# Seven weight tiles of a one-core mixture-of-experts kernel move by 32 to 416 bytes

## The chip, the cores and the metric

The kernel runs on one core of a Trainium2 chip. The metric is the device time of one execution in microseconds; lower is better. In the rows, PE is the matrix engine (TensorE), PEld its weight loads, DVE the vector engine, ACT the scalar engine, POOL GpSimd, SP the engine that issues most transfers.

## The reference, cut to what matters

```python
x = retention(q, k, v)             # 2304 tokens x 512, decayed causal attention without softmax
P = sinkhorn(exp(x @ w_gate))      # 8 rounds of row and column scaling, 2304 x 8
for e in range(8):                 # first layer: every token through every expert
    out += P[:, e:e+1] * (relu(x @ w1[e]) @ w2[e])      # w1 512 x 1024, w2 1024 x 512
logits = out @ moe2_w_gate         # second layer: only the expert with the largest logit
out2[t] = softmax(logits[t])[e] * (relu(out[t] @ w1b[e]) @ w2b[e])
```

## The kernel before, in words

Four stages follow one another: the attention, pass 1 of the first layer, pass 2 of it, and the second layer (class `Top1`). In pass 1 and pass 2 a unit `u` is half of one expert (512 of its 1024 hidden columns), so there are 16 units in each pass. Every factor is split into a high and a low part (`...h`, `...l`, 32-bit), and a product is taken as three matmuls: high with high, low with high, high with low.

The hidden layer of one unit, for 1024 tokens, is made by `Dense.hidden` with seven block products in place of eight. Product `i` multiplies the weight block `w{a}` with the token block `op{b}`, where `PROD` gives `(a, b)`. A weight tile is 128 x 2 x 256 values, 2048 bytes in each of the 128 rows of the on-chip memory; a token tile is 128 x 1024, 4096 bytes. `product` issues six matmuls for each of two column blocks `p`: two depth halves `k`, three matmuls in each. The weights (128 columns, 512 bytes a row) are loaded into the array, and 512 token columns (2048 bytes a row) stream past them. Every matmul brings its own weight load. Per unit these are 7 x 2 x 6 = 84 matmuls, so 2688 over the 32 units. They write `pha`, `phb` and `phc` (L609).

In pass 1, 256 further tokens use the same weight tiles in `rest_hidden` (`phr`, L706, 256 columns, 48 matmuls a unit, 768 in all). `y_tile` (L731) then multiplies the hidden values with `w2`: here a 128-column slice of `hhi` or `hlo` is the weight and `w2hi` or `w2lo` streams, 512 columns at a time.

All tiles of the seven products come out of pools that are laid one behind another. Before the change, `op0h` to `op6l`, `w0h` to `w6l`, `w2hi`, `w2lo`, `hhi`, `hlo`, `xrh`, `xrl`, `rhi` and `rlo` all begin at an address that is 480 modulo 512 bytes, so that a weight tile and the tokens that stream past it are a multiple of 512 bytes apart. Small unused tiles (`pad0` to `pad3`) hold this.

`lg` holds the first layer's logits (128 x 18 x 8). `sinkhorn` reads it at the start of pass 1. `Router.L` (named `L2` in its pool) holds the second layer's logits; `logit_parts` writes it 128 tokens at a time in pass 2, and `choose` and `gates` read it.

Of the kernel before, what the change touches and what calls it, by code (L numbers as in the profile page):

```python
# [10 lines left out]
F32 = mybir.dt.float32  # L11
F32R = mybir.dt.float32r
# [11 lines left out]
E = 8  # L24
F = 1024
NPAIR = H // 2
NT = N // 128
# [10 lines left out]
def split_lo(eng, out, src, hi):  # L38

    return eng.tensor_tensor(out=out, in0=src, in1=hi.bitcast(F32), op=ALU.subtract)  # L40
# [345 lines left out]
class Pumped:  # L386


    def __init__(self, eng):
        self.eng, self.bg = eng, []  # L390
# [121 lines left out]
class Dense:  # L512
# [35 lines left out]

    def w1_tasks(self, u):
        nc = self.nc  # L550
        ops = self.W1[u] = [
            tuple(self.w1p.tile([128, 2, 256], F32R, name=f"w{o}{x}", tag=f"w{o}{x}") for x in "hl")
            for o in range(7)
        ]

        def q(f, k):
            return self.raw1[:, 2 * k:2 * k + 2, 256 * f:256 * f + 256]

        def split(o, f, k):
            def run():  # L560
                nc.scalar.activation(ops[o][0], q(f, k), AF.Copy)  # L561
                split_lo(nc.vector, ops[o][1], q(f, k), ops[o][0])
            return run

        def comb(out, a, b, op):
            def run():
                nc.vector.tensor_tensor(out=q(*out), in0=q(*a), in1=q(*b), op=op)  # L567
            return run

        a11, a12, a21, a22 = (0, 0), (0, 1), (1, 0), (1, 1)  # L570
        return [
            split(A11, *a11), split(A12, *a12), split(A22, *a22),
            comb(a22, a21, a22, ALU.add), split(S1, *a22),
            comb(a21, a11, a21, ALU.subtract),
            comb(a11, a22, a11, ALU.subtract), split(S2, *a11), split(S3, *a21),
            comb(a12, a12, a11, ALU.subtract), split(S4, *a12),
        ]
# [206 lines left out]
class Router:  # L784
# [5 lines left out]

    def __init__(self, tc, ctx, crow, ident, wg2, acc, x2d, res, pt):
        self.tc, self.nc, self.ident, self.acc, self.pt = tc, tc.nc, ident, acc, pt
        self.x2d, self.res = x2d, res
        nc = self.nc
        self.v = Pumped(nc.vector)
        self.pool = pool = ctx.enter_context(tc.tile_pool(name="r_sb", reuse_waits="tile", bufs=1))
        self.C = pool.tile([128, CKEEP], F32, name="crow")
        nc.scalar.dma_start(self.C, crow[:, 0:CKEEP])  # L800
        self.wg = pool.tile([128, KD, E], F32, name="wg2")
        nc.scalar.dma_start(self.wg, wg2.rearrange("(k p) e -> p k e", p=128))
        self.C16 = pool.tile([128, 3, 128], BF16, name="c16")
        with tc.tile_pool(name="r_c", reuse_waits="tile", bufs=1) as tmp:
            t = tmp.tile([128, 384], F32, name="crow_b")
            nc.scalar.dma_start(t, crow[:, CKEEP:CKEEP + 384])
            nc.vector.tensor_copy(self.C16.rearrange("p a b -> p (a b)"), t)
        self.L = pool.tile([128, NT, E], F32, name="L2")
        self.Bm = pool.tile([128, NT, 128], BF16, name="Bm")
        self.q = pool.tile([128, NT], F32, name="rq")  # L810
        self.gp = pool.tile([128, 3, NT], BF16, name="gparts")
        self.oh = [pool.tile([128, E, n], BF16, name=f"oh{n}") for n in (NEARLY, NLATE)]
        self.xt = pool.tile([128, KD, 128], F32, name="rxt")
        pool.tile([128, 8], F32, name="pad3")
        self.B = [{}, {}]

    def c(self, k):
# [518 lines left out]
def build(ctx, tc, q, k, v, moe_w_gate, moe_w1, moe_w2, moe2_w_gate, moe2_w1, moe2_w2,  # L1336
# [4 lines left out]
    x2d = dram.tile([N, DM], F32, name="x2d")  # L1341
# [3 lines left out]
    ident = const.tile([128, 128], F32, name="ident")  # L1345
    const.tile([128, 8], F32, name="pad1")
    make_identity(nc, ident)
    res = {
        "gidx0": const.tile([128, 2], U32, name="gidx0"),
        "gidx": const.tile([128, NSLOT], U32, name="gidx"),  # L1350
        "sidx": const.tile([128, NSLOT], U32, name="sidx"),
        "gate": const.tile([128, NSLOT], F32, name="gate"),
        "e0": const.tile([128, 1], I32, name="e0"),
        "eidx": const.tile([128, NSLOT], I32, name="eidx"),
        "echg": const.tile([128, NSLOT], I32, name="echg"),
        "nslot": const.tile([128, 1], I32, name="nslot"),
# [3 lines left out]
    lg = const.tile([128, NT, E], F32, name="lg")  # L1360
# [3 lines left out]
    ops = [tuple(xpool.tile([128, 1024], F32R, name=f"op{o}{x}") for x in "hl") for o in range(7)]  # L1364
# [31 lines left out]
    with ExitStack() as cx:  # L1396
# [19 lines left out]
        aux = ctx.enter_context(tc.tile_pool(name="aux", reuse_waits="tile", bufs=1, space=PSUM))  # L1416
# [35 lines left out]
    with tc.manual_schedule(engines=order):  # L1452
# [3 lines left out]
        for u in range(2 * E):  # L1456
# [20 lines left out]
            if u == 2 * E - 1:  # L1477
# [8 lines left out]
                g, w = nc.gpsimd, nc.vector  # L1486
# [17 lines left out]
                    t()  # L1504


        ro = Router(tc, ctx, c_row, ident, moe2_w_gate, acc, x2d, res, aux)
        etmp = ctx.enter_context(tc.tile_pool(name="r_early", reuse_waits="tile", bufs=1))
        for i in range(NEARLY):
            ro.store(i)  # L1510
# [53 lines left out]
    with tc.manual_schedule(engines=MANUAL):  # L1564
# [58 lines left out]
    n = nc.values_load(  # L1623
        res["nslot"][0:1, 0:1], min_val=NFULL, max_val=NSLOT,
        skip_runtime_bounds_check_because="18 to 26 slots hold 2304 tokens of 8 experts",
    )
# [40 lines left out]
```

## Time and profile before

| | |
|---|---|
| median of three runs | 2007.47 us (2002.96 to 2007.79) |
| the profiled execution's own time | 2002.13 us |
| its span, first to last instruction | 2000.3 us |
| TensorE clock granted, mean | 0.996 of 2.4 GHz |
| PE busy | 1956.9 us, 98% of the span, 9584 matmuls |
| PEld busy | 1627.4 us, 81% |
| DVE, ACT, POOL busy | 1252.1, 847.7, 298.9 us |

Matmuls are pipelined: one starts before the one ahead of it has ended, and the duration that a row gives for one (389 ns for 512 columns) is longer than the distance from its start to the next one's. What a matmul costs in a dense stretch is that distance. It is read from the start times, or from a stretch of the chain of waits divided by its count.

### The profile page before, as it was taken

To read this page: it belongs to the slowest core of one execution; us is meant where nothing else is said; L and a number is where in the kernel's file an instruction comes from. 1 tells how busy PE (TensorE), PEld (TensorE's weight loads), DVE (VectorE), ACT (ScalarE), POOL (GpSimd) and SP (SyncE) were. 2 spreads that over 40 slices of the span, in tenths; PEclk is the share of its full clock that TensorE was granted. 3 is DMA by queue.
4 is the path that set the end of the run, shared out by engine and by line. 5 is a ranking of instruction groups with operands and counts; after the bars stand their busy time and mean duration, and the time that the engine had idled before them with its cause. 6 is when DMAs were issued, how large, how long until landed. Compare 5 with 4: busy or idle time off the path is not lost.

```text
span 2000.3 us, 25444 instructions
## 1 busy us (share of the span) xinstructions
PE 1956.9 (98%) x9584; PEld 1627.4 (81%) x9584; DVE 1252.1 (63%) x2059; ACT 847.7 (42%) x1454; POOL 298.9 (15%) x250
## 2 busy tenths in 40 slices
PE   8989999999999999999999999999999999999997
PEld 7777888888888888888878888888878888777775
DVE  7897565555555555555455556555576654988886
ACT  6665424232222233323333333333333334577785
POOL 6572000000000000000000000000000001465654
PEclk9999999999999999999999999999999999999998
DMA  5621111111111110111311111111111113112755
GB/s 132 142 61 64 42 43 43 43 43 43 43 42 43 43 37 28 42 43 43 111 33 64 43 43 64 42 54 52 43 46 60 47 59 116 43 43 77 249 200 192
DMA packets 112111, 134.94 MB, mean 67 GB/s; under 512 B 62190, under 2 KB 62446, under 8 KB 111600
## 3 DMA queue, kind: packets, MB, share of 16 engines
q1 hardware_dynamic: 106960, 121.92, 19.0%
q0 software_dynamic: 3680, 11.02, 1.7%
q8 instruction: 77, 1.26, 0.3%
q10 hardware_dynamic: 1344, 0.33, 0.1%
q14 instruction: 50, 0.41, 0.1%
HBM read 182.53 MB, written 12.58 MB: 98 GB/s over the span
## 4 chain that ended last, share of the span: by engine, by line
PE 82%; DVE 8%; ACT 5%; issue 3%; DMA 1%; POOL 0%; SPq 0%; ACTq 0%; POOLq 0%; DVEq 0%
PE pyt L731 37%; PE pha L609 17%; PE phc L609 8%; PE phr L706 5%; PE phb L609 4%; PE phs L1250 4%; DVE op2l L40 2%; PE po L274 2%; PE ps L210 1%; ACT op3h L1216 1%; PE pS L236 1%; ACT op2h L1216 1%; PE rpl L832 1%; DMA raw<-in_moe_w_dram 1%; PE pgate L1381 1%
## 5 line engine op out<-in xcount | busy, mean ns | idle before, releaser
L731 PE MATMUL pyt<-w2hi,hhi 128*128 128x512 f32 x1024 | 402.5, 393 | 2.4 <-DVE xb L742 2.2
L731 PE MATMUL pyt<-w2hi,hlo 128*128 128x512 f32 x1024 | 398.9, 390 | 0.0
L731 PE MATMUL pyt<-w2lo,hhi 128*128 128x512 f32 x1024 | 398.5, 389 | 0.0
L635 ACT ACTIVATE q<-pha 128x512 f32<-128x512 f32 x192 | 114.7, 599 | 266.8 <-PE pha L609 264.4
L623 ACT ACTIVATE hhi<-q 128x512 fp32r<-128x512 f32 x192 | 121.4, 632 | 249.9 <-DVE q L631 249.9
L731 PEld LDWEIGHTS pyt<-w2hi,hhi 128*128 128x128 f32 x1024 | 192.3, 188 | 42.8 <-DVE xb L742 2.9
L731 PEld LDWEIGHTS pyt<-w2hi,hlo 128*128 128x128 f32 x1024 | 192.2, 188 | 40.7
L731 PEld LDWEIGHTS pyt<-w2lo,hhi 128*128 128x128 f32 x1024 | 192.4, 188 | 38.8
L624 DVE SCALAR_TENSOR_TENSOR hlo<-q,hhi 128x512 fp32r<-128x512 f32 x192 | 133.0, 693 | 96.8 <-ACT hhi L623 90.8
L742 DVE SCALAR_TENSOR_TENSOR xa<-pyt,P,xa 128x512 f32<-128x512 f32 x140 | 105.0, 750 | 136.0 <-PE pyt L731 135.2
L742 DVE SCALAR_TENSOR_TENSOR xb<-pyt,P,xb 128x512 f32<-128x512 f32 x120 | 90.1, 751 | 94.0 <-PE pyt L731 94.0
L631 DVE TENSOR_TENSOR q<-phb,q 128x512 f32<-128x512 f32 x64 | 44.3, 692 | 166.0 <-PE phb L609 166.0
L40 POOL TENSOR_TENSOR op2l<-xb,op2h 128x1024 fp32r<-128x1024 f32 x1 | 2.4, 2387 | 719.4 <-ACT op2h L494 719.4
L631 DVE TENSOR_TENSOR q<-phc,q 128x512 f32<-128x512 f32 x128 | 87.8, 686 | 34.0 <-PE phc L609 33.1
L561 ACT ACTIVATE w3h<-raw 128x512 fp32r<-128x512 f32 x31 | 19.6, 631 | 160.4 <-DVE raw L567 160.3
L567 DVE TENSOR_TENSOR raw<-raw 128x512 f32<-128x512 f32 x124 | 85.1, 687 | 1.1
L40 DVE TENSOR_TENSOR w2lo<-raw,w2hi 128x512 fp32r<-128x512 f32 x124 | 84.6, 683 | 0.0
L587 ACT ACTIVATE w2hi<-raw 128x512 fp32r<-128x512 f32 x124 | 77.1, 623 | 0.0
L714 DVE SCALAR_TENSOR_TENSOR rlo<-phr,rhi 128x512 fp32r<-128x512 f32 x32 | 22.1, 691 | 87.7 <-ACT rhi L713 87.7
L908 POOL TENSOR_SCALAR Bm<-c,ro 128x128 bf16<-128x128 bf16 x2 | 1.3, 653 | 456.2 <-DVE ro L408 456.2
L561 ACT ACTIVATE w4h<-raw 128x512 fp32r<-128x512 f32 x31 | 19.6, 632 | 116.2 <-DVE raw L567 116.2
L40 DVE TENSOR_TENSOR op2l<-raw,op2h 128x1024 fp32r<-128x1024 f32 x22 | 60.6, 2756 | 10.1 <-ACT op2h L1216 9.6
(391 smaller groups left out, 4765.3 us busy)
## 6 DMA issues: line engine op xcount, KB each, us to landing
raw<-in_moe_w_dram SPq DMA_DIRECT2D x180, 512.0 KB
raw<-in_moe_w_dram SPq DMA_DIRECT2D x62, 1024.0 KB
kt<-in_k_dram SPq DMA_DIRECT2D x32, 128.0 KB
vt<-in_v_dram SPq DMA_DIRECT2D x32, 128.0 KB
qt<-in_q_dram SPq DMA_DIRECT2D x32, 128.0 KB
x2d<-xa SPq DMA_DIRECT2D x10, 256.0 KB
xbd<-xb SPq DMA_DIRECT2D x1, 2048.0 KB
xb<-xbd SPq DMA_DIRECT2D x2, 1024.0 KB
```

Source lines behind the costliest of these rows:

```text
L40: return eng.tensor_tensor(out=out, in0=src, in1=hi.bitcast(F32), op=ALU.subtract)
L567: nc.vector.tensor_tensor(out=q(*out), in0=q(*a), in1=q(*b), op=op)
L587: nc.scalar.activation(hi, self.raw2[:, fc, :], AF.Copy)
L609: self.nc.tensor.matmul(bank, ww[:, k, 128 * p:128 * p + 128], xx[:, k, :], start=start and n == 0, stop=stop and n == 5, skip_group_check ...
L623: nc.scalar.activation(hi, c, AF.Relu)
L624: nc.vector.scalar_tensor_tensor(out=lo, in0=c, scalar=0.0, in1=hi.bitcast(F32), op0=ALU.max, op1=ALU.subtract)
L631: self.nc.vector.tensor_tensor(out=s, in0=p, in1=s, op=ALU.add)
L635: self.nc.scalar.activation(t, c, AF.Copy)
L706: nc.tensor.matmul(pt[:, j, :], w[:, k, 128 * j:128 * j + 128], xr[x][:, xi, k, :], start=n == 0, stop=n == 11,)
L731: nc.tensor.matmul(pt, hh, ww, start=n == 0, stop=n == 11)
L742: nc.vector.scalar_tensor_tensor(out=acc, in0=pt, scalar=P[:, i, e:e + 1], in1=acc, op0=ALU.mult, op1=ALU.add)
L1250: nc.tensor.matmul(ph, xx[:, k, :], ww[:, fs], start=n == 0, stop=n == 11)
```

## The change

Eight unused tiles are laid around the seven weight pairs. They hold 8, 8, 8, 24, 16, 16, 24 and 24 values of 4 bytes, so 32, 32, 32, 96, 64, 64, 96 and 96 bytes, 512 in all. A pair takes 4096 bytes, eight times 512, so the distance modulo 512 from a weight tile to its tokens becomes the sum of the unused tiles ahead of it:

| weight | w0 | w1 | w2 | w3 | w4 | w5 | w6 |
|---|---|---|---|---|---|---|---|
| product, tokens | 1, op0 | 2, op1 | 4, op6 | 5, op3 | 6, op4 | 7, op5 | 3, op2 |
| distance before | 0 | 0 | 0 | 0 | 0 | 0 | 0 |
| distance after, bytes | 32 | 64 | 96 | 192 | 256 | 320 | 416 |

To make room, the second layer's logits no longer have a tile of 576 bytes of their own; they are written into `lg`, and `pad3` grows by 64 bytes, so what follows the router's pool stays at its place modulo 512. No instruction is added, removed or moved on any engine, and no wait: the two programs differ in addresses, and in the name of the logits' tile.

```diff
     def w1_tasks(self, u):
         nc = self.nc
-        ops = self.W1[u] = [
-            tuple(self.w1p.tile([128, 2, 256], F32R, name=f"w{o}{x}", tag=f"w{o}{x}") for x in "hl")
-            for o in range(7)
-        ]
+        ops = self.W1[u] = []
+
+        for o, n in enumerate((8, 8, 8, 24, 16, 16, 24, 24)):
+            self.w1p.tile([128, n], F32, name=f"pad{o}", tag=f"pad{o}")
+            if o < 7:
+                ops.append(tuple(
+                    self.w1p.tile([128, 2, 256], F32R, name=f"w{o}{x}", tag=f"w{o}{x}") for x in "hl"
+                ))
...
-        self.L = pool.tile([128, NT, E], F32, name="L2")
+        self.L = L
...
-        pool.tile([128, 8], F32, name="pad3")
+        pool.tile([128, 24], F32, name="pad3")
...
-        ro = Router(tc, ctx, c_row, ident, moe2_w_gate, acc, x2d, res, aux)
+        ro = Router(tc, ctx, c_row, ident, moe2_w_gate, acc, x2d, res, aux, lg)
```

## Rows read from the trace of the kernel before

**Rows 1.** The page: the span, busy time of each engine.

```profile
span 2000.3 us, 25444 instructions
PE 1956.9 (98%) x9584; PEld 1627.4 (81%) x9584; DVE 1252.1 (63%) x2059; ACT 847.7 (42%) x1454; POOL 298.9 (15%) x250
```

**Rows 2.** The page: the chain that ended last, shares by engine and line.

```profile
PE 82%; DVE 8%; ACT 5%; issue 3%; DMA 1%; POOL 0%; SPq 0%; ACTq 0%; POOLq 0%; DVEq 0%
PE pyt L731 37%; PE pha L609 17%; PE phc L609 8%; PE phr L706 5%; PE phb L609 4%; PE phs L1250 4%; DVE op2l L40 2%; PE po L274 2%; PE ps L210 1%; ACT op3h L1216 1%; PE pS L236 1%; ACT op2h L1216 1%; PE rpl L832 1%; DMA raw<-in_moe_w_dram 1%; PE pgate L1381 1%
```

**Rows 3.** Busy time by stage: pass 1, pass 2 (columns: see first line).

```profile
core 0: us, PE busy (x) PEld busy (x) DVE busy (x) ACT busy (x) POOL busy (x), PEclk, DMA share, GB/s
190.00:1020.00 830.00, 828.70 (x4006) 699.74 (x4005) 449.08 (x725) 260.09 (x445) 10.38 (x11) 1.00 0.14 46
1020.00:1675.00 655.00, 652.38 (x2957) 540.35 (x2956) 379.97 (x608) 240.01 (x422) 2.66 (x3) 1.00 0.16 54
```

**Rows 4.** Chain of waits, one unit of pass 1 (start us, us, what).

```profile
410.99 27.20 PE pyt L731 x120
438.19 2.72 PE pha L609 x12
440.91 1.36 PE phb L609 x6
...
449.07 2.87 PE phr L706 x24
451.94 2.75 PE phc L609 x12
454.69 2.72 PE pha L609 x12
...
463.03 1.13 PE pyt L731 x5
```

**Rows 5.** Chain of waits, a part of one unit of pass 2.

```profile
1041.60 13.76 PE pyt L731 x60
1055.36 2.72 PE pha L609 x12
```

**Rows 6.** Timeline of PE after a break in pass 2 (start us, duration us).

```profile
1041.78 0.40 PE L731 MATMUL pyt<-w2lo,hhi 128*128 128x512 f32 x1
1042.02 0.40 PE L731 MATMUL pyt<-w2hi,hlo 128*128 128x512 f32 x1
1042.25 0.40 PE L731 MATMUL pyt<-w2hi,hhi 128*128 128x512 f32 x1
...
1044.10 0.39 PE L731 MATMUL pyt<-w2hi,hlo 128*128 128x512 f32 x1
```

**Rows 7.** Timeline of the weight loads at the same place.

```profile
1041.78 0.19 PEld L731 LDWEIGHTS pyt<-w2hi,hlo 128*128 128x128 f32 x1
1042.02 0.19 PEld L731 LDWEIGHTS pyt<-w2hi,hhi 128*128 128x128 f32 x1
```

**Rows 8.** Line 609: duration ns min/median/max (two of 21 alike).

```profile
L609 PE MATMUL pha<-op4h,w4l x128: 389/389/398, 182.0 to 1648.9; 128*128 128x512 f32 x128
L609 PE MATMUL pha<-op5h,w5h x128: 389/389/389, 185.9 to 1652.7; 128*128 128x512 f32 x128
```

**Rows 9.** Line 731, 1041.7 to 1043.9 us: duration ns min/median/max.

```profile
L731 PE MATMUL pyt<-w2hi,hhi x4: 393/397/486, 1041.5 to 1043.6; 128*128 128x512 f32 x4
L731 PE MATMUL pyt<-w2lo,hhi x4: 387/389/396, 1041.8 to 1043.9; 128*128 128x512 f32 x4
L731 PE MATMUL pyt<-w2hi,hlo x3: 393/395/397, 1042.0 to 1043.4; 128*128 128x512 f32 x3
```

**Rows 10.** Line 1250, from 1750 us, and `op2l`, which it waits for.

```profile
L1250 PE MATMUL phs<-op2h,xth x34: 388/388/389, 1754.1 to 1965.9; 128*128 128x512 f32 x34
L1250 PE MATMUL phs<-op2l,xth x34: 389/442/504, 1755.1 to 1966.1; 128*128 128x512 f32 x34
```

**Rows 11.** Line 1381 (8-column weights), two forms; line 706.

```profile
L1381 PE MATMUL pgate<-xa,wg x8: 379/379/383, 129.7 to 131.2; 128*8 128x256 f32 x8
...
L1381 PE MATMUL pgate<-xb,wg x16: 592/592/596, 164.8 to 177.9; 128*8 128x512 f32 x16
...
L706 PE MATMUL phr<-xrh,w0h x64: 277/283/283, 188.6 to 971.1; 128*128 128x256 f32 x64
```

**Rows 12.** Tiles `lg` and `L`: last reading of one, first writing of the other.

```profile
L427 DVE TENSOR_SCALAR sk_x<-lg,gm x1: 296/296/296, 186.0 to 186.0; 128x144 f32<-128x144 f32 x1
...
L833 ACT ACTIVATE L<-rpl x18: 158/178/179, 1042.0 to 1699.2; 128x8 f32<-128x8 f32 x18
```

**Rows 13.** The page: the two groups with the longest waits for PE.

```profile
L635 ACT ACTIVATE q<-pha 128x512 f32<-128x512 f32 x192 | 114.7, 599 | 266.8 <-PE pha L609 264.4
L623 ACT ACTIVATE hhi<-q 128x512 fp32r<-128x512 f32 x192 | 121.4, 632 | 249.9 <-DVE q L631 249.9
```

More of the change, by code (lines that the diff above doesn't have):

```diff
@@ L784, with __init__ @@
 class Router:
-    def __init__(self, tc, ctx, crow, ident, wg2, acc, x2d, res, pt):
+    def __init__(self, tc, ctx, crow, ident, wg2, acc, x2d, res, pt, L):
         self.tc, self.nc, self.ident, self.acc, self.pt = tc, tc.nc, ident, acc, pt
```

## The prediction

> **What bounds the kernel now.** I read the page first. PE is busy for 1956.9 of 2000.3 us [rows 1], and 82% of the chain that ended last is PE's; the lines of the seven products (`pha`, `phc`, `phb`) hold 17, 8 and 4% of the span, and `phr`, which shares their weights, another 5% [rows 2]. The stages come next: in pass 1 PE is busy for 828.7 of 830.0 us, in pass 2 for 652.4 of 655.0, with the granted clock at 1.00, which is the 2.4 GHz level [rows 3]. So nothing that DVE, ACT or a transfer does sets the pace there. The rows with the longest waits say the same from the other side: ACT sits idle for 264.4 us until a `pha` product is done, and 249.9 us for `q`, which DVE makes from a product [rows 13]. A nanosecond more or less in a product's matmul is therefore a nanosecond of the end, 2688 times over, and nothing covers it.
>
> What does such a matmul cost? The chain in order of time gives it for a whole unit: 120 matmuls of `pyt` in 27.20 us, 12 of `pha` in 2.72, 6 of `phb` in 1.36 [rows 4]. Each is 226.7 ns from start to start. Products and `pyt` cost the same; all of them stand at distance 0.
>
> Then I looked for places where the same matmul costs something else, since the change moves only the place of the weights. There are such places, after a break. In pass 2, behind the small matmuls of the router, ten starts of `pyt` go from 1041.78 to 1044.10 [rows 6]: 232 ns each, though nothing is waited for. The durations there lie at 387 to 397 ns [rows 9] (the 486 is the first one, whose next weights came late). In the products the median is 389, and the maximum where the flow was not broken is 389 too, else up to 398 [rows 8]. So a matmul has a quiet state, in which it stays once it is there, and a restless one that lasts some ten matmuls after a break. What runs beside it is the next weight load, which starts with it, to the 10 ns of the rows [rows 6, 7]. Where no weight load runs beside it, the duration is 388: at line 1250 `op2h` with `xth` comes just before a wait for `op2l`, and 34 of these read 388, 388, 389 [rows 10]. I read from this that a weight load and the tokens that stream at the same time can hinder each other by up to 10 ns in 389, that it depends on how they lie to each other in time, and that at distance 0 the flow settles where it costs 1 ns.
>
> **The change part by part.** *The weights' new distances.* No instruction is added. A matmul streams 512 columns in about 213 ns (the step from 256 to 512 columns of `pgate`, whose operands take two steps a column, is 592 less 379 ns for 512 steps [rows 11]), so a distance of 32 to 416 bytes, 8 to 104 columns, is 3 to 43 ns of the stream. The quiet and the restless state differ by less than that. So I take it that each distance puts the load and the stream into another relation, and that the quiet one is not to be expected by chance. No row shows a 128-column weight of these products at another distance, so the price is bounded:
>
> - dearest: every product matmul as in the longest row, 398 against 389, so 9 ns more: 2688 x 9 = 24 us.
> - nothing: the flow settles again at any distance.
> - a gain, near: the shortest row, 387 against 389: 2688 x 2 = 5 us less.
> - a gain, far: if weights of 8 columns show what a stream costs unhindered, 379 ns for the same 512 steps [rows 11], then 10 ns less: 2688 x 10 = 27 us less. The 388 of the lone matmuls speaks against it: without a load beside it, the time did not fall to 379.
>
> I take the restless mean, 232 - 226.7 = 5.3 ns, because it is a mean over several relations, as seven distances are: 2688 x 5.3 = 14.2 us.
>
> *The tokens of `rest_hidden`.* `phr` uses w0 to w3 past `xr`, 768 matmuls at 2.87 us for 24 [rows 4], 119.6 ns each. Its first of a group takes 277, all others 283, and 283 is the most too [rows 11]. Bounds: 6 ns less each, 4.6 us, to nothing; I take nothing, since all that follow the first sit at 283, the dear end.
>
> *The way back.* `pyt` keeps distance 0, but has to settle again behind restless products. What that costs is seen where `phc` follows `phr`: 2.75 us against 2.72 for the same count [rows 4], 0.03 us. Once a unit, 32 x 0.03 = 1 us. (Behind the router it is more: 13.76 us for 60 [rows 5] against 60 x 0.2267 = 13.60, 0.16, of which about 0.1 is the late first weight load.)
>
> *The shared tile.* `lg` is last read at 186.0 us, and the first logits of the second layer are written at 1042.0 [rows 12], 856 us later; the vector engine's reading is long over, so writing to it waits for nothing. Cost: nothing, and if it did wait it would be the 178 ns of a copy on ACT, which is idle then.
>
> Sum: 14.2 + 0 + 1 + 0 = 15 us. Against the profiled execution's own 2002.1 us this gives 2017; the median of the runs is 5.3 us higher, and on it the sum gives 2022.5. The profiled execution lies below all three runs, so I lean to the median, and say 2020.
>
> **The rivals.** *No change.* The quiet state comes from the time at which a load starts, not from addresses: `pyt`, whose weights and moving operand stand in other pools, settles at the same 226.7 as the products. Then the flow settles at every distance and the time stays at 2007. Speaking for it: after every break in the trace the flow settles within some ten matmuls. Against it: all of these are at distance 0, so they don't show whether another would settle. The Trainium skill has a rule that says this more strongly: "TensorE: Matmul & The Clock Gate", Part 2, step 1, gives PE two independent read ports, so that loading the next weights takes no read bandwidth from the running matmul. By that rule the sum would be 0 and the time 2007; the trace agrees for the quiet state (389 beside 388), and not for the restless one (up to 398).
>
> *Settling at each change of distance.* The flow settles, but each product begins anew. By the order in `hidden` the distance changes new to the flow are seven in a unit of pass 1 (from `pyt` to w0, then w1, w4, w1, w5; w3 to w2; w6 to `pyt`; behind `phr` it settles anew already) and nine in one of pass 2, which has no `phr`: 16 x 7 + 16 x 9 = 256, at the 0.03 us of `phc` 7.7 us, so 2015. It lies just above what a measurement can tell.
>
> *Faster.* At distance 0 the load and the stream read the same bytes modulo 512 at nearly the same time; if that is the dear relation and the others are free, each matmul falls towards 379, which is 10 ns less. With all seven distances 27 us are gained: 1980; with two of them 7.7 us: 2000. It decides from a fall of 2.3 ns in the mean (6 us over 2688). For it: the 10 ns that separate the 8-column weights from the others. Against it: the restless matmuls pass through many relations and none is shorter than 387.
>
> **How the numbers follow.** Restless products, 2020: 0.42. Settling at each change, 2015: 0.15. No change: 0.31. Faster: 0.12. Two runs of this kernel can be told apart from about 0.3%, 6 us. The first case is slower by more than that but for about a tenth of it, the second in two of three cases, and a change that is called none strays beyond 6 us seldom, to either side: slower 0.50, same 0.38, faster 0.12. The range goes from 2001 (no change, at its low end) to 2034 (the dearest row on the median, 2032, with the way back); below it lies most of the faster case, above it a hindrance larger than any row shows. The first case alone would be 2013 to 2034.
>
> **What would show it.** In the chain of one unit in pass 1, `pha` x12 should go from 2.72 to about 2.78 us, and `pyt` x120 stay at 27.20 to 27.25. In the durations by line, the products should stand at medians that differ by weight, between 387 and 398, with all matmuls of one weight alike. If all medians are 389 and `pha` x12 is 2.72, the relation is one of time alone, and the first step is wrong. If a distance shows less than 387, the bound from the restless rows is wrong. If `pyt` or the attention changes instead, the cause is not the distance of the products. And if the end moves while the products' rows don't, look at the second layer, whose tiles all lie 512 bytes lower.

## The result, and the profile after

The changed kernel takes 2017.64 us (median) against 2003.08 for the kernel before in the same runs. One of its five executions took 3560.9 us, at a granted clock of 0.766 where the others show 0.993 to 0.996, and is left out of the ratio. The ratio is 1.0057, with an interval of 1.0043 to 1.0072. It goes by means, 2016.0 us against 2004.7, and so lies below what the two medians would give. That is 11.4 us slower (8.6 to 14.4, the ratio less one, times 2003). The profiled execution has a span of 2012.7 us, 12.4 us more than before.

The page's first lines show PE with the same number of matmuls and 12.9 us more of busy time [rows 1]; the weight loads, DVE, ACT and POOL stay where they were, within 0.7 us:

```profile
span 2012.7 us, 25444 instructions
PE 1969.8 (98%) x9584; PEld 1626.7 (81%) x9584; DVE 1252.4 (62%) x2059; ACT 847.4 (42%) x1454; POOL 299.2 (15%) x250
```

The chain of waits of the changed kernel, one unit of pass 1 (start us, us, what), answers to [rows 4]:

```profile
412.36 27.25 PE pyt L735 x120
439.60 2.79 PE pha L613 x12
442.39 1.40 PE phb L613 x6
443.79 2.75 PE pha L613 x12
...
447.94 2.80 PE pha L613 x12
450.74 2.83 PE phr L710 x24
453.57 2.74 PE phc L613 x12
456.31 2.81 PE pha L613 x12
...
461.96 2.80 PE phc L613 x12
464.76 3.44 PE pyt L735 x15
```

The order of products gives the distances: 2.79 is w0 at 32 bytes, 1.40 (for six) w1 at 64, 2.75 w4 at 256, 2.80 w5 at 320, 2.74 w3 at 192, 2.81 w2 at 96, 2.80 w6 at 416. Before, 12 matmuls took 2.72. `pyt`, whose tiles did not move, takes 27.25 for 27.20, and `phr` less than before: 2.83 for 2.87. From the first product to the next `pyt` it is 25.16 us (464.76 - 439.60) where it was 24.84 (463.03 - 438.19, [rows 4]).

In pass 2, where no `phr` lies between, the same stretch is 19.51 us (from the two starts below) where 84 matmuls at the 2.72 of [rows 5] make 19.04:

```profile
1060.84 2.79 PE pha L613 x12
...
1080.35 4.13 PE pyt L735 x18
```

So a unit loses 0.32 + 0.05 us in pass 1 and 0.47 in pass 2. Sixteen of each would be 13.4 us, which is 1.0 more than the span grew, since the two units shown stand for the others only roughly. Added up from the start times of all matmuls in the two traces, the stretches of the seven products grow by 13.5 us, those of `pyt` by 0.3, and those of `phr` shrink by 1.3. That makes 12.6, against the 12.4 of the span, with nothing left over for the shared tile.

The durations by line of five of the seven low weights, and of w3's high one (ns min/median/max), answer to [rows 8]:

```profile
L613 PE MATMUL pha<-op0h,w0l x128: 392/396/502, 172.8 to 1656.9; 128*128 128x512 f32 x128
...
L613 PE MATMUL phb<-op1h,w1l x128: 392/396/398, 180.4 to 1662.4; 128*128 128x512 f32 x128
...
L613 PE MATMUL pha<-op4h,w4l x128: 389/391/395, 181.8 to 1661.1; 128*128 128x512 f32 x128
...
L613 PE MATMUL phc<-op3h,w3h x128: 388/388/398, 191.3 to 1667.8; 128*128 128x512 f32 x128
L613 PE MATMUL phc<-op3h,w3l x128: 392/392/394, 191.6 to 1668.0; 128*128 128x512 f32 x128
...
L613 PE MATMUL pha<-op6h,w2l x128: 392/396/400, 194.3 to 1670.8; 128*128 128x512 f32 x128
```

The reader is to see the minimum as well as the median: with the low weights at 32, 64, 96 and 192 bytes no single one of the 128 matmuls reached the 389 that was the median of all before. Of the five, only w4, at 256, still does. Not every matmul is longer, though: with w3's high weight, at 192, the first matmul of a group stands at 388, and the next one at 392. What has grown is the sum over a group.

### The profile page after: what moved, and what is told of

Same layout as the page of the kernel before. It is cut to its first block, busy times and chain, and to the rows that moved or that the text cites. A ratio compares the mean times of both kernels' runs of the same rounds, so it can differ in the third digit from the quotient of the medians.

```text
span 2012.7 us, 25444 instructions
## 1 busy us (share of the span) xinstructions
PE 1969.8 (98%) x9584; PEld 1626.7 (81%) x9584; DVE 1252.4 (62%) x2059; ACT 847.4 (42%) x1454; POOL 299.2 (15%) x250
## 4 chain that ended last, share of the span: by engine, by line
PE 82%; DVE 8%; ACT 4%; issue 3%; DMA 1%; POOL 1%; SPq 0%; ACTq 0%; POOLq 0%; DVEq 0%
PE pyt L735 37%; PE pha L613 17%; PE phc L613 8%; PE phr L710 5%; PE phb L613 4%; PE phs L1254 4%; DVE op2l L40 2%; PE po L274 2%; PE ps L210 1%; PE pS L236 1%; ACT op3h L1220 1%; ACT op2h L1220 1%; PE rpl L836 1%; ACT op0h L1220 1%; PE pgate L1385 1%
```

## The experiments

The theory on record: the weights and what streams past them hinder each other, by an amount that depends on their distance, and away from 0 the flow does not come to rest. The rivals: the distance does nothing (the place, the shared tile or the shift of later tiles does); or each change of distance costs one settling and no more. All kernels compute the same as the changed one. Where eight sizes of unused tiles are given, they replace `(8, 8, 8, 24, 16, 16, 24, 24)`, and an unused tile of size 0 is left out.

**The shared tile, and nothing else.**

```diff
-        for o, n in enumerate((8, 8, 8, 24, 16, 16, 24, 24)):
+        for o, n in enumerate((128, 0, 0, 0, 0, 0, 0, 0)):
```

> The logits share the dead tile and the same 512 bytes are spent, but as one unused tile ahead of w0, so all seven distances stay 0 modulo 512. If the distances are the cause: the time of before, 2003 us within 6, and pha x12 at 2.72 us in the chain. If the shared tile, or the shift of everything behind the weights by 512 bytes, is the cause: the time of the change, near 2015.

Measured: 2002.49 us, ratio 0.9995 (0.9983 to 1.0007), and in the chain of waits:

```profile
443.37 2.72 PE pha L614 x12
```

The 512 bytes are spent and the logits share `lg`, and the time is that of before. These parts of the change cost nothing, so what is left is the place of the weights.

**Another place, the same distances.** All of TensorE's tiles move by 96 bytes modulo 512, left and right pools alike.

```diff
-    const.tile([128, 88], F32, name="pad0")
+    const.tile([128, 112], F32, name="pad0")
...
+        pool(ctx, "b_pad", bufs=1, side="right").tile([128, 104], F32, name="pad4")
         self.hp = pool(ctx, "b_h", bufs=8, side="right")
...
-        for o, n in enumerate((8, 8, 8, 24, 16, 16, 24, 24)):
+        for o, n in enumerate((0, 0, 0, 0, 0, 0, 0, 0)):
```

> All tiles that TensorE reads begin 96 bytes further modulo 512 (64 in place of 480), and all distances stay 0. If the distance between the weights and what streams past them decides: the time of before, 2003 us within 6, products and pyt at 226.7 ns. If the place itself (480 modulo 512) was the good one: products, pyt and the second layer all slower, some 5 ns on 2688 + 3456 + 1055 matmuls, 36 us, near 2039.

Measured: ratio 1.0001 (0.9988 to 1.0014). The chain of waits reads as before, line by line:

```profile
412.21 27.20 PE pyt L737 x120
...
443.49 2.72 PE pha L615 x12
...
450.29 2.87 PE phr L712 x24
453.16 2.75 PE phc L615 x12
```

So 480 modulo 512 is no better a place than 64. With the first experiment, that leaves the distance.

**One distance for all seven weights.** Five kernels, each with sizes of the form `(d/4, 0, 0, 0, 0, 0, 0, (512 - d)/4)`. At 256:

```diff
-        for o, n in enumerate((8, 8, 8, 24, 16, 16, 24, 24)):
+        for o, n in enumerate((64, 0, 0, 0, 0, 0, 0, 64)):
```

> All seven weights at distance 256. In the changed kernel the product at 256 (w4) cost 2.75 us for 12, 2.5 ns more each than before. If each distance has a price of its own that lasts: 2688 x 2.5 ns = 7 us, near 2010. If a flow settles at any distance and only the change of distance costs: only the two changes a unit to and from pyt and phr remain, 32 x 2 x 0.03 = 2 us, near 2005, and pha x12 at 2.72.

at 64:

> All seven weights at distance 64. In the changed kernel the product at 64 (w1) cost 1.40 us for 6, 6.6 ns more each. If each distance has a price that lasts: 2688 x 6.6 ns = 18 us, near 2021, with pha x12 at 2.80. If a flow settles at any distance: near 2005, and pha x12 at 2.72.

at 128:

> All seven weights at distance 128, which no kernel has had yet. If what settles repeats every 128 bytes: as at 0 and 256, 2003 us, pha x12 at 2.72. If it repeats every 256 bytes: another price that lasts, between those of 192 and 64, 7 to 17 us, 2010 to 2020, with pha x12 at 2.75 to 2.80.

at 192:

> All seven weights at distance 192. In the changed kernel w3 at 192 went through starts 226, 229 and 232 ns apart, again and again, 229.2 in the mean. If that lasts: 2688 x 2.5 ns = 7 us, near 2010. If it was on its way to rest: near 2004.

and at 320:

> All seven weights at distance 320, which is 64 more than 256. If 256 bytes are the whole of the pattern: the price of 64, 17 us, near 2020, starts 231 and 236 ns apart in turn, and pha x12 at 2.80. If the pattern takes 512 bytes and 256 was good by chance: another price and another sequence.

Measured, against the kernel before on the same chip; the last two columns are the chain of waits of one unit of pass 1 (us):

| distance | median us | ratio | interval | `pha` x12 | `phr` x24 |
|---|---|---|---|---|---|
| 64 | 2019.78 | 1.0077 | 1.0052 to 1.0103 | 2.80 | 2.83 |
| 128 | 2017.37 | 1.0068 | 1.0052 to 1.0085 | 2.78 to 2.79 | 2.84, 2.88 |
| 192 | 2007.28 | 1.0021 | 1.0011 to 1.0031 | 2.75 | 2.83 |
| 256 | 2002.49 | 0.9994 | 0.9982 to 1.0005 | 2.72 | 2.87 |
| 320 | 2019.96 | 1.0078 | 1.0061 to 1.0095 | 2.80 | 2.83 |

As ratio less one, times 2003, these are 15.4 us at 64 (18 on record), 13.6 at 128 (7 to 17), 4.2 at 192 (7), nothing at 256 (7 if the price lasted, 2 if not) and 15.6 at 320 (17).

The rows behind four of them. The chain at 256 bytes, at 64, at 192 and at 320, in this order, with one stretch of `pha` and, but for 256, the `phr` behind it:

```profile
447.71 2.72 PE pha L614 x12
```

```profile
448.23 2.80 PE pha L614 x12
451.03 2.83 PE phr L711 x24
```

```profile
447.42 2.75 PE pha L614 x12
450.16 2.83 PE phr L711 x24
```

```profile
452.38 2.80 PE pha L614 x12
455.18 2.83 PE phr L711 x24
```

and the durations of the same matmul (ns min/median/max) at 256, 64, 320 and 128:

```profile
L614 PE MATMUL pha<-op5h,w5h x128: 389/389/389, 187.3 to 1654.7; 128*128 128x512 f32 x128
```

```profile
L614 PE MATMUL pha<-op5h,w5h x128: 393/396/398, 185.7 to 1666.9; 128*128 128x512 f32 x128
```

```profile
L614 PE MATMUL pha<-op5h,w5h x128: 392/396/399, 189.9 to 1670.9; 128*128 128x512 f32 x128
```

```profile
L614 PE MATMUL pha<-op5h,w5h x128: 390/394/404, 189.7 to 1669.3; 128*128 128x512 f32 x128
```

At 256 all 128 of these matmuls take 389, as at 0. At 64 none of them is below 393, though the distance is the same through whole units and there is nothing new to settle to: the price lasts. At 320 it is the price of 64. So what counts, as far as these six distances (0 with them) show, repeats every 256 bytes and not only every 512; two pairs, 0 with 256 and 64 with 320, are all that shows it. 128 is not enough of a step, since there the time is 13.6 us longer (0.0068 x 2003). At 192 the price lasts too, at 2.75 against 2.72, but is small.

A lasting price does not mean that the flow finds no rest. At 192 the three matmuls of a group take nearly the same three values each time, and at 64 the shorter `phr` matmuls stand at one value, 281, where they stood at 283 before [rows 11]:

```profile
L614 PE MATMUL pha<-op5h,w5h x128: 388/392/392, 186.9 to 1657.7; 128*128 128x512 f32 x128
L614 PE MATMUL pha<-op5h,w5l x128: 392/394/394, 187.1 to 1658.0; 128*128 128x512 f32 x128
L614 PE MATMUL pha<-op5l,w5h x128: 388/388/394, 187.3 to 1658.2; 128*128 128x512 f32 x128
```

```profile
L711 PE MATMUL phr<-xrh,w0h x64: 281/281/281, 188.5 to 977.3; 128*128 128x256 f32 x64
```

**Changes of distance alone.** w1, w2 and w3 at 256, the others at 0.

```diff
-        for o, n in enumerate((8, 8, 8, 24, 16, 16, 24, 24)):
+        for o, n in enumerate((0, 64, 0, 0, 64, 0, 0, 0)):
```

> w0, w4, w5, w6 at distance 0, w1, w2, w3 at 256, so the distance changes six times in a unit of pass 1, always between the two that settle. If a change of distance costs something by itself: 32 units x 6 x 0.03 us = 6 us, near 2009. If only the distance counts, and 0 and 256 are the same: 2003 us within 3, and pha x12 at 2.72 everywhere.

Measured: ratio 0.9996 (0.9986 to 1.0006).

```profile
442.04 1.36 PE phb L614 x6
443.40 2.72 PE pha L614 x12
446.12 1.36 PE phb L614 x6
447.48 2.72 PE pha L614 x12
```

Between `phb` (w1, 256) and `pha` (w4 and w5, 0) the distance changes each time, and no stretch is longer than before. A change of distance between two quiet ones costs nothing.

**The other line of matmuls.** The seven products stand at 0; `w2hi` and `w2lo`, which stream in `pyt`, are moved, so that the weights there stand at 64 from them.

```diff
+        pool(ctx, "b_pad", bufs=1, side="right").tile([128, 16], F32, name="pad4")
         self.w2p = pool(ctx, "b_w2", bufs=4, side="right")
+        pool(ctx, "b_pad2", bufs=1, side="right").tile([128, 112], F32, name="pad5")
         self.w1p = pool(c1, "b_w1", bufs=1, side="right")
...
-        for o, n in enumerate((8, 8, 8, 24, 16, 16, 24, 24)):
+        for o, n in enumerate((0, 0, 0, 0, 0, 0, 0, 0)):
```

> The seven products stand at distance 0; instead the w2 tiles that stream in pyt are moved, so that the weights there (slices of hhi, hlo, rhi, rlo) stand at distance 64 from them. If the rule is of TensorE and not of the products: 3456 matmuls x 6.5 ns = 22 us, 2025, with pyt at 231 and 236 ns in turn and pha x12 at 2.72 (pyt x120 near 28.0 us in the chain). If it is of the products' tiles alone: 2003.

Measured: 2024.14 us, ratio 1.0104 (1.0087 to 1.0121), 20.8 us (22 on record). The program has two instructions more, both waits; the kernel whose tiles all moved has the same two, and there they cost nothing. The chain, and the durations of one kind of `pyt`:

```profile
415.37 28.00 PE pyt L738 x120
443.36 2.74 PE pha L616 x12
```

```profile
L738 PE MATMUL pyt<-w2hi,rhi x128: 393/394/395, 203.8 to 1001.6; 128*128 128x512 f32 x128
```

120 matmuls take 28.00 us, 233.3 ns each, as the products do at 64. So the price is not one of the products' tiles alone, and it is paid with the tiles of the moving side displaced, too. The starts were expected 231 and 236 ns apart in turn; in the trace they are 233 or 234 apart, and the durations keep to 393 to 395. This flow is about as even as the one at 0, and dearer. The 2.74 of the first `pha`, for 2.72 of those after it, is the settling behind a stretch at 64: 0.02 us.

**Only one half of the weights.** The low weights at 64 and the high ones at 0; then the mirror.

```diff
+        hs = row("h")      # all seven; in the mirror ls comes first
+        self.w1p.tile([128, 16], F32, name="pad0", tag="pad0")
+        ls = row("l")
+        self.w1p.tile([128, 112], F32, name="pad1", tag="pad1")
+        ops = self.W1[u] = list(zip(hs, ls))
```

> The high weights at distance 0, the low ones at 64. Of the three matmuls of a group (high with high, low with high, high with low tokens), the low weights are loaded while the first streams, and are used in the second. If the load of the next weights and the tokens streaming beside it hinder each other: the first matmul of a group is the long one, and one in three matmuls at most carries the 6.6 ns of distance 64 directly, so 2 to 3 ns in the mean and 2008 to 2011, if the other two do not settle. If it is a matmul's own weights against its own tokens: the second is the long one, at the same sum. If only a flow with all weights at one distance can be restless: 2003.

> The mirror of the kernel with the low weights at 64: the high weights at 64, the low ones at 0. There the second matmul of a group, with the low weights, took 397 and the others 392 and 389. If a matmul's own weights against its own tokens decide: now the first and third are long and the second short. If the weights loaded beside it decide: the second and third are long (the high weights of the next matmul are loaded beside them) and the first short. The mean should lie above the 231.0 ns of the mirror and below the 233.3 of all at 64: 12 to 18 us, 2015 to 2021.

Measured: ratio 1.0054 (1.0037 to 1.0071) for the first, 1.0051 (1.0031 to 1.0071) for the mirror; `pha` x12 is 2.77 us in both. The durations of the three matmuls of a group, low weights at 64:

```profile
L613 PE MATMUL pha<-op5h,w5h x128: 392/392/392, 187.0 to 1662.1; 128*128 128x512 f32 x128
L613 PE MATMUL pha<-op5h,w5l x128: 397/397/398, 187.2 to 1662.3; 128*128 128x512 f32 x128
L613 PE MATMUL pha<-op5l,w5h x128: 389/389/389, 187.5 to 1662.5; 128*128 128x512 f32 x128
```

and of the mirror, with the third of a group (low tokens) from w0:

```profile
L613 PE MATMUL pha<-op5h,w5h x128: 390/398/398, 187.0 to 1662.3; 128*128 128x512 f32 x128
L613 PE MATMUL pha<-op5h,w5l x128: 393/394/399, 187.2 to 1662.6; 128*128 128x512 f32 x128
```

```profile
L613 PE MATMUL pha<-op0l,w0h x128: 387/388/398, 174.3 to 1654.5; 128*128 128x512 f32 x128
```

These two were to tell whether a matmul is hindered by its own weights' distance or by that of the weights that are loaded beside it, and they don't. With the low weights displaced, the order is 392, 397 and then 389; in the mirror 398, 394, 388. The first fits "own weights" by its longest one; the mirror fits neither, since its third matmul uses displaced weights and has displaced weights loaded beside it, and is the shortest. Both sums also miss: I had 2 to 3 ns in the mean for the first and measured 4.1 (2.77 us for 12, less 226.7), and 12 to 18 us for the mirror and measured 10.2. The third case on record, that only a flow with all weights at one distance pays, is excluded by both ratios. Single matmuls can't be read alone: with all weights at 64 one and the same pair, w5 with `op5h`, reads 393 at one time and 398 at another. In both programs some waits stand at other places, too, as in the kernel whose tiles all moved, where that cost nothing.

## Why the prediction was right, and where it was not

The direction held, and so did the path: the products' own matmuls, in both passes, by an amount that goes with the distance. 15 us were worked out, 11.4 measured (8.6 to 14.4), 12.4 in the profiled spans, so the sum was somewhat too dear. The forecast of 2020 stands 2.4 us from the median and 4.0 from the mean, 2016.0. The range, 2001 to 2034, holds the times of three of the four cases, so that the time lies in it says little; its upper end is 1 us above what it was made of (2032 and 1).

*"Restless products."* This part of the mechanism held only in part. The prediction took it that away from 0 the matmuls go on ranging, as they do behind a break. With all at 64 they do range, those of w5 over 393 to 398, and with all at 128 over 390 to 404. But at 192, in `pyt` at 64 and with the low weights alone at 64 they keep to nearly fixed values (392, 397 and 389 in the last), and the price is paid all the same. So what the runs show is a longer mean spacing at a bad distance, whether it ranges or not. The sign that all matmuls of one weight would be alike was missed, too: those of w3 stand at 388 and 392.

*The restless mean, 5.3 ns.* In pass 2 the products measure 19.51 us for 84, 232.3 ns, so 5.6 more than before. That the ten matmuls behind a break came so near was luck for the most part: they all stood at distance 0, and nothing tied their mean to that of seven distances. The uniform kernels show 0 to 6.6 ns a matmul (2.72 to 2.80 us for 12), and another set of seven, nearer to 0 and 256, would have cost little.

*"The quiet one is not to be expected by chance."* Of six distances, 0 and 256 are quiet and 192 nearly so. The product at 256, w4, paid 2.75 in the changed kernel and 2.72 when all stood there: its share was the settling alone, behind w1 at 64, since a change between 0 and 256 costs nothing. So the rival "settling at each change" is right in part for this one product and wrong for the sum: at 64 bytes everywhere, with no change to settle to, the time is 15.4 us longer (0.0077 x 2003).

*Nothing for `phr`.* Too dear by 1.1 us: 2.83 and 2.84 for 2.87 in a unit (450.74 in the rows of after), 0.07 us a unit, 16 units. I held 283 ns for its dear end and took it as the place where it would stay; away from 0 and 256 it left it, to the cheap side. At 64 the 256-column matmuls stand at 281 and the 512-column ones at 393 to 398, where 0 gives 283 and 389: the distance that is dear for the one is cheap for the other.

*The way back, 1 us.* 27.25 for 27.20 us of `pyt` in pass 1: 0.8 us in 16 units, and no more in pass 2 (13.72 us for 60, against 13.76 in [rows 5]). By the start times of both passes it was 0.3.

*The shared tile, nothing.* Shown by the first experiment.

*The 388 of matmuls without a load [rows 10].* The prediction gives all 34 as standing just before a wait. In this stretch `op2l` was waited for 17 times; the 17 matmuls before these waits take 388, and the other 17 have the next load beside them and take 389. The difference of 1 ns stands, on half the rows.

*The bounds.* The dearest row, 398, was passed by one median (399, w2's high weight with the low tokens); single matmuls reached 400 at 96 bytes and 405 at 128. The near gain was not seen: no distance tried was faster than 0. The base was the weak term: I put the sum on a median of three runs, 2007.5, and the same kernel has medians of 2003.1 to 2003.4 in the later comparisons.

*The rule of the Trainium skill* ("TensorE: Matmul & The Clock Gate", Part 2, step 1: two independent read ports, the next weights' load takes no read bandwidth from the running matmul) was taken to give 0 us. The measurement differs from that: 64 bytes of distance between the same tiles cost 15.4 us, with the instructions and waits of the kernel with all at 0 and `lg` shared. It fits the flow at 0 and 256 bytes, where a matmul beside a load takes 389 ns, and one alone at 0 takes 388. What is refuted is the 0 us; whether the load takes anything from the matmul is not shown, as the next paragraph says.

Left open: what it is that the weights' place disturbs. That the load of the next weights is the partner was read from the time at which it starts, and the 388 of matmuls without one [rows 10]; the two kernels with half the weights displaced did not confirm a pairing. A row of the traces speaks against it. In pass 2 one `phb` is the last matmul before a wait, and the next load comes over 1.3 us after its start, at distance 0 (first line) and with all at 128 (second line):

```profile
L609 PE MATMUL phb<-op1l,w1h x1: 388/388/388, 1015.1 to 1015.1; 128*128 128x512 f32 x1
```

```profile
L614 PE MATMUL phb<-op1l,w1h x1: 397/397/397, 1025.2 to 1025.2; 128*128 128x512 f32 x1
```

It is the longer at 128 though no load runs beside it. As it is one matmul in each trace, and the end of a matmul is modelled in these rows, this is a hint and not a proof. Only 0, 64, 128, 192, 256 and 320 bytes were tried for all weights; 32, 96 and 416 stood in the changed kernel alone, and no other distance was tried.

## What to carry to other kernels

In a dense stretch of matmuls that each bring their own 128-column 32-bit weights, lay the tiles so that weights and streamed operand are a multiple of 256 bytes apart: up to 3% of every matmul of 512 columns (2.80 against 2.72 us for 12) hung on it here, and no instruction shows it. When PE is busy all the time, a duration's minimum, median and maximum by line tell more than its mean. One value throughout is not yet a good one: 392 and 397 stood nearly unmoved in a kernel that was 0.5% slower. Compare it with the shortest that the same shape reaches elsewhere. The matmuls behind a break show how much there may be to lose, here 5.3 ns each, before anything is changed; they don't give the price of any one distance, which was between 0 and 6.6.

## What the runs showed of the hardware that was not expected

Distance 256 is as good as 0 (ratio 0.9994), and 320 costs what 64 does (1.0078, 1.0077). The price does not wear off within a dense stretch: 120 matmuls of `pyt` at 64 bytes take 28.00 us, ten times the 2.80 of 12. A flow can be even and dear: 393 to 395 in `pyt` at 64 against 389 at 0. For 256 columns it is the other way round: `phr` x24 takes 2.83 us at 64, 192 and 320 bytes, 2.84 and 2.88 at 128, and 2.87 at 0 and 256.
